# A chunked-attention kernel with two expert layers: the third tile moved ahead of two second halves, and one layer's block sums gathered in the sixth tile

## The chip, the cores and the metric

The kernel runs on one core of a Trainium2 chip. The metric is the device time of one execution in microseconds (us). TensorE (PE in the profile) multiplies matrices, VectorE (DVE), ScalarE (ACT) and GpSimd (POOL) compute element by element, SyncE (SP) issues transfers, and the DMA engines carry them. Each engine works through its own instructions in order; semaphores tie them together.

## What is computed

Attention within chunks of 64 positions, then two layers over its 4608 tokens. Weights come as float64.

```python
scores = scale * np.matmul(q_c, k_c.transpose(0, 1, 2, 4, 3))
scores = scores - np.max(scores, axis=-1, keepdims=True)
attn = np.exp(scores)
attn = attn / (np.sum(attn, axis=-1, keepdims=True) + 1e-09)
x = np.matmul(attn, v_c)          # -> 4608 x 512
...
h = x @ w_in                      # 512 x 2048
x = (h * np.cos(h)) @ w_out       # 2048 x 512
...
h = x @ w_in2                     # 512 x 1024
solu = h * softmax(h)
ln = (solu - mu) / np.sqrt(var + 1e-06) * g_ln
out = ln @ w_out2                 # 1024 x 512
```

## The kernel before

**Tiles, units and steps.** The tokens form nine tiles of 512. Attention is done in units: 0 to 3 (two chunks each) make tile 0, units 4 and 5 (four chunks each) tile 1, units 6 and 7 tile 2, and so on. A unit's output is x of its half tile, kept as a high and a low part (xh, xl), since a product of float32 precision is built from three matmuls of split operands. Two tiles of x fit in SBUF at a time (pool xp, 2 buffers).

Layer 1 runs in steps (j, f): tile j, and one of 16 blocks f of 128 columns of w_in. `mm_in` makes h of the step (12 matmuls), ACT and DVE make g = h cos h of it (`turns`: kt on ACT, r on DVE; `act_sin`: two passes on ACT; `dve_g`; `split_g`: gh on ACT, gl on DVE or POOL), and `mm_out` multiplies it with a block of w_out into y, two steps later (LAG 2). h has two PSUM buffers, so that h of step n + 2 goes where h of step n was, once g of step n is made. The order of the steps is the list `blocks`: before, tiles 0 and 1 do their first eight blocks each, then tile 0 the second eight, then tile 1, then tiles 2 to 8 all sixteen each. Step 85 is thus the sixth block of the sixth tile. A tile whose blocks are done in two halves keeps its partial y in DRAM meanwhile (`load_part` brings it back).

**What sets the order.** All instructions of PE, ACT, DVE, POOL and SP keep the order in which the program writes them (`InOrder`). Up to step 33 that is a list of words written by hand: h.3 is `mm_in(3)`, k, r, s, g, c, b or d the parts of a step's g, y.n and z.n the two halves of `mm_out(n)`; capital letters are pieces of a unit's attention (S.4 are the scores of unit 4, Tk its key transposes), lt, lv, lq load it; i1bH is a pass over the second half of pair 1 of w_in's blocks (H and W make the high and low parts, the other letters convert from float64), o0H one of w_out; wi, wo, li, lo load raw weights, and n.k are k warm-up matmuls on an identity, which compute nothing that is used. From step 34 on, a step has eight slots (e, p1, y, a1, d1, p2, a2, d2), and `plan` puts work into a slot of a step:

```python
def step(n):
    mm_in(n); run(n, "e"); turns(n); split_g(n - 1); run(n, "p1"); mm_out(n - LAG); run(n, "y")
    run(n, "a1"); run(n, "d1"); act_sin(n); dve_g(n); run(n, "p2"); run(n, "a2"); run(n, "d2")
```

`place` puts units 8 to 17 there; a unit's `load_next`, in slot p2, issues the q and k transfers of the unit after it: 32 transfers of 32 KB on SP. SP's transfers use eight semaphores in turn, and each one waits until the transfer eight before it has landed.

**Layer 2** multiplies x @ w_in2 by seven products of quarter blocks in place of eight, so it wants sums of w_in2's blocks. w_in2 is converted in the tiles 2 and 3 and put in DRAM (w2f0, w2f1: two halves kk of its rows). Then `load_blk(kk)` reads one half back (wf), `blk_sum` makes the sums s1 to s4 on DVE, and `keep` splits each of the seven blocks w11, w12, w22, s1 to s4 into a high part (an ACT pass, half 0) and a low part (a DVE pass, half 1) and stores both from a half e of the tile wk to DRAM, w2_<name>. A half of wk is written again only when the store before has read it. Before, kk = 0 is done in tile 4 and kk = 1 in tile 5.

Of the kernel before, what the change touches and what calls it, by code (L numbers as in the profile page):

```python
# [11 lines left out]
F32 = mybir.dt.float32  # L12
F32R = mybir.dt.float32r
# [15 lines left out]
def kernel(  # L29
# [13 lines left out]
    B, H, S, D = q.shape  # L43
# [3 lines left out]
    P = 128  # L47
    CH = 64
    T = 512
    NJ = NT // T  # L50
    SUB = T // P
    NI = NT // P
    KD = DM // P
    NF = F1 // P
# [8 lines left out]
    dr = ctx.enter_context(tc.tile_pool(name="dr", bufs=1, space=DRAM))  # L63
# [10 lines left out]
    NB = 8  # L74

    N32 = NB
    blocks = [(0, 0, NB), (1, 0, NB), (0, NB, NF), (1, NB, NF)]
    blocks += [(j, 0, NF) for j in range(2, NJ)]
    steps = [(j, f) for j, f0, f1 in blocks for f in range(f0, f1)]
    heads = {(j, f0) for j, f0, f1 in blocks}  # L80
    tails = {(j, f1 - 1) for j, f0, f1 in blocks}
    y_part = [dr.tile([P, KD * T], F32, name=f"yp{j}") for j in range(2)]
    y_dram = [dr.tile([2, P, 7 * 256], F32, name=f"yd{j}") for j in range(NJ)]

    xp = ctx.enter_context(tc.tile_pool(name="xp", bufs=2))
# [27 lines left out]
    sync = InOrder(nc.sync, in_order_loads)  # L113
# [110 lines left out]
    def load_w2in(g):  # L224
        t = sp_.tile([P, 1024], U64, tag="st", name="st")
        sync.dma_start(out=t, in_=w_in2[g * P:(g + 1) * P, :])
        raw["in2", g] = t
# [29 lines left out]
    def load_blk(kk):  # L257
        t = sp_.tile([P, 2048], F32, tag="st", name="wf")
        sync.dma_start(out=t, in_=w2f[kk])
        blk[kk] = t, zp.tile([P, 1024], F32, tag="z", name="z"), sp_.tile([P, 2048], F32R, tag="st", name="wk")  # L260
# [144 lines left out]
    def warm(n):  # L405

        t = ps_h.tile([P, P], F32, tag="h", name="none")
        for _ in range(n):
            pe.matmul(out=t, lhsT=ident, rhs=ident, start=True, stop=True)

    def att_tok(i, w):

# [170 lines left out]
    xh, xl = {}, {}  # L583
# [102 lines left out]
    def load_part(j):  # L686
        t = sp_.tile([P, KD, T], F32, tag="st", name="yp")
        sync.dma_start(out=t.rearrange("p m t -> p (m t)"), in_=y_part[j])
        parts[j] = t
# [75 lines left out]
    if True:  # L765
# [48 lines left out]
        for i in range(SUB, NU):  # L814
            j, o = divmod(UNITS[i][0] * CH, T)
# [3 lines left out]
        def plan(n, when, what):  # L819
            att.setdefault((n, when), []).append((lambda i: what(), NU))  # L820

        def conv_at(key, places):
            for (e, k), (n, when) in zip(((0, 0), (0, 1), (0, 2), (1, 0), (1, 1), (1, 2)), places):
                plan(n, when, lambda e=e, k=k: conv(key, e, k))

        for t in (2, 3):
            o = NF * t
            for x in range(2):
                plan(o + 5, "p2", lambda g=2 * x + t - 2: load_w2in(g))
            conv_at(("in2", t - 2), ((o + 7, "a2"), (o + 8, "d2"), (o + 9, "d2"), (o + 8, "a2"), (o + 10, "d1"), (o + 12, "d1")))  # L830
            conv_at(("in2", t), ((o + 13, "a1"), (o + 13, "d1"), (o + 13, "d2"), (o + 13, "a2"), (o + 14, "d2"), (o + 16, "d1")))
        for t in (4, 5):
            o, kk = NF * t, t - 4
            plan(o + 5, "p2", lambda kk=kk: load_blk(kk))
            for what, key, e, n, x in (
# [3 lines left out]
            ):  # L839
                if what == "s":  # L840
                    plan(o + n, f"d{x}", lambda kk=kk, key=key: blk_sum(kk, key))
                else:
                    plan(o + n, f"a{x}", lambda kk=kk, key=key, e=e: keep(kk, e, key, 0))
                    plan(o + n, f"d{x}", lambda kk=kk, key=key, e=e: keep(kk, e, key, 1))
        for t in (6, 7):
            o = NF * t
            for x in range(2):
                g = 2 * (t - 6) + x
                plan(o + 5, "p2", lambda g=g: load_w2out(g))
            g = 2 * (t - 6)  # L850
# [11 lines left out]
        def half_out(n, m):  # L862
# [20 lines left out]
            "Ck": lambda i: att_tokc(i, 1), "S": att_qk, "M": att_max, "U": att_sub, "E": att_exp,  # L883
            "R": att_sum, "L": att_mul, "P": att_pt, "D": att_ptc, "V": att_pv,
            "XH": lambda i: att_x(i, 0), "XL": lambda i: att_x(i, 1),
            "n": warm,
            "nq": lambda i: att_nat(i, "q"), "nk": lambda i: att_nat(i, "k"),
            "cq": lambda i: att_natc(i, "q"), "ck": lambda i: att_natc(i, "k"),
            "tq": lambda i: att_tr(i, "q"), "tk": lambda i: att_tr(i, "k"),
# [223 lines left out]
        BEFORE = 34  # L1113
        ordered[0] = True
        for word in (
# [26 lines left out]
        ).split():  # L1142
            if word == "|":
                first.close()
                cp = act_a.enter_context(tc.tile_pool(name="cp", bufs=2, reuse_waits="tile"))
            else:
                say(word)
# [20 lines left out]
        for n in range(BEFORE - 1, END):  # L1168
            j, f = steps[n - LAG]
# [46 lines left out]
        for i in range(EARLY, NI // 2 + (LAG2 + 1) // 2 + 1):  # L1216
            p, t = i - 1, 2 * i - LAG2
# [98 lines left out]
```

## Time and profile before

| | us |
|---|---|
| median of three runs | 1255.84 |
| runs | 1254.85, 1255.84, 1256.05 |
| profiled execution | 1254.68 |
| its span in the trace | 1252.9 |
| PE busy | 1241.4 (99%) |
| VectorE busy | 862.4 (69%) |
| ScalarE busy | 751.7 (60%) |
| GpSimd busy | 130.0 (10%) |
| mean granted TensorE clock | 0.998 |

The span is the time from the first to the last instruction in the trace; about 1.8 us of the execution lie around it. The granted clock is a share of TensorE's full 2.4 GHz; 0.5 is its other level, 1.2 GHz. Busy time is the sum of an engine's instructions; a row's bracket gives the idle time just before an instruction and what released it. SPq is SP's sequencer, on which an issue takes time from when it may start until it is handed over.

### The profile page before, as it was taken

The page shows a single profiled execution, that of the slowest core. Times are in us where ns is not written, and L with a number is a line of the kernel's source. Part 1 is how long each engine was busy: PE and PEld are TensorE (multiplying, and loading weights), DVE is VectorE, ACT ScalarE, POOL GpSimd, SP SyncE. Part 2 cuts the span into 40 slices and gives each one's busy share as a digit, 9 for nine tenths or more (in the row PEclk, how much of TensorE's full clock was granted, in tenths as well). Part 3 has the DMA queues.
Part 4 walks back from the last instruction along what each step waited for, and adds up shares of the span by engine and source line. Part 5 has one row for each costly group of instructions (what it writes and reads, how often), then busy time and mean ns, then how long its engine had stood idle before and what let it go on. Part 6 is the DMA issues. An engine that isn't in the chain of part 4 may idle for free.

```text
span 1252.9 us, 20476 instructions
## 1 busy us (share of the span) xinstructions
PE 1241.4 (99%) x7636; PEld 1012.5 (81%) x7636; DVE 862.4 (69%) x1390; ACT 751.7 (60%) x1108; POOL 130.0 (10%) x216
## 2 busy tenths in 40 slices
PE   8999999999999999999999999999999999999998
PEld 7767888888888888888888888888888888888887
DVE  5968875666766766667667757647689777777761
ACT  5968865555645645646646547537666655656552
POOL 1213322011011011011011011000000000000010
PEclk9999999999999999999999999999999999999999
DMA  9952152463263254354373371561556543454325
GB/s 226 276 138 101 58 135 57 114 171 74 54 176 66 58 144 128 85 136 130 80 169 76 85 160 51 194 221 60 164 142 180 129 125 108 121 152 122 75 50 120
DMA packets 249476, 153.95 MB, mean 123 GB/s; under 512 B 180001, under 2 KB 223521, under 8 KB 247585
## 3 DMA queue, kind: packets, MB, share of 16 engines
q1 hardware_dynamic: 245824, 148.32, 45.8%
q0 software_dynamic: 3456, 4.20, 1.5%
q8 instruction: 60, 0.98, 0.4%
q14 instruction: 40, 0.32, 0.1%
q10 hardware_dynamic: 96, 0.13, 0.0%
HBM read 85.73 MB, written 41.68 MB: 102 GB/s over the span
## 4 chain that ended last, share of the span: by engine, by line
PE 96%; ACT 1%; SPq 1%; DMA 1%; DVE 0%; issue 0%; ACTq 0%; DVEq 0%
PE h L104 44%; PE y L104 32%; PE o L104 15%; PE sc L104 2%; PE x L104 2%; SPq L104 1%; DMA qki<-in_k 0%; PE none L104 0%; PE kt L431 0%; PE qt L431 0%; PE pt L104 0%; DMA yd<-ye 0%; PE qkt L104 0%; SPq L1063 0%; ACT lh L104 0%
## 5 line engine op out<-in xcount | busy, mean ns | idle before, releaser
L104 PE MATMUL h<-xh,whi 128*128 128x512 f32 x576 | 229.4, 399 | 0.1
L104 PE MATMUL h<-xl,whi 128*128 128x512 f32 x576 | 224.0, 390 | 0.0
L104 PE MATMUL h<-xh,wlo 128*128 128x512 f32 x576 | 223.9, 390 | 0.0
L104 ACT ACTIVATE kt<-h 128x512 int32<-128x512 f32 x144 | 85.7, 595 | 225.6 <-PE h L104 224.6
L104 PE MATMUL y<-gh,whi 128*128 128x512 f32 x544 | 212.6, 391 | 0.0
L104 PE MATMUL y<-gl,whi 128*128 128x512 f32 x544 | 211.7, 389 | 0.0
L104 PE MATMUL y<-gh,wlo 128*128 128x512 f32 x544 | 211.7, 389 | 0.0
L104 ACT ACTIVATE r<-r 128x512 f32<-128x512 f32 x288 | 181.7, 631 | 47.5 <-DVE r L104 42.9
L104 DVE SCALAR_TENSOR_TENSOR r<-kt,h 128x512 f32<-128x512 int32 x144 | 98.6, 685 | 151.1 <-ACT kt L104 150.9
L104 DVE SCALAR_TENSOR_TENSOR g<-r,h 128x512 f32<-128x512 f32 x136 | 92.7, 681 | 56.0 <-ACT r L104 55.8
L104 PEld LDWEIGHTS h<-xh,whi 128*128 128x128 f32 x576 | 108.0, 188 | 26.0 <-issue 1.6
L104 PEld LDWEIGHTS h<-xh,wlo 128*128 128x128 f32 x576 | 108.2, 188 | 23.3 <-issue 1.2
L104 PEld LDWEIGHTS h<-xl,whi 128*128 128x128 f32 x576 | 108.1, 188 | 22.8
L104 PEld LDWEIGHTS y<-gh,whi 128*128 128x128 f32 x544 | 102.1, 188 | 21.5
L104 PEld LDWEIGHTS y<-gh,wlo 128*128 128x128 f32 x544 | 102.1, 188 | 21.3
L104 PEld LDWEIGHTS y<-gl,whi 128*128 128x128 f32 x544 | 102.1, 188 | 21.0
L104 PE MATMUL o<-whi,lh 128*128 128x512 f32 x288 | 112.0, 389 | 0.0
L104 PE MATMUL o<-wlo,lh 128*128 128x512 f32 x288 | 112.0, 389 | 0.0
L104 PE MATMUL o<-whi,ll 128*128 128x512 f32 x288 | 112.0, 389 | 0.0
L104 ACT ACTIVATE gh<-g 128x512 fp32r<-128x512 f32 x136 | 84.8, 624 | 23.7 <-DVE g L104 17.9
L533 POOL DMA_DIRECT2D ptb<-ptr x96 | 47.2, 499 | 495.4 <-DVE ptr L526 463.1
L104 PE MATMUL h<-whi,yl 128*128 128x512 f32 x252 | 98.2, 390 | 0.2 <-DVE yl L104 0.2
(112 smaller groups left out, 1953.5 us busy)
## 6 DMA issues: line engine op xcount, KB each, us to landing
lt<-bt SPq DMA_DIRECT2D x136, 128.0 KB
yr<-yd SPq DMA_DIRECT2D x18, 896.0 KB
yd<-ts SPq DMA_DIRECT2D x18, 512.0 KB
out<-os SPq DMA_DIRECT2D x142, 64.0 KB
vi<-in_v SPq DMA_DIRECT2D x64, 128.0 KB
qi<-in_q SPq DMA_DIRECT2D x224, 32.0 KB
ki<-in_k SPq DMA_DIRECT2D x224, 32.0 KB
raw<-in_moe_w_in SPq DMA_DIRECT2D x10, 512.0 KB
```

The source lines that it names most:

```text
L104: ins = getattr(self.engine, name)(*args, **kwargs)
L533: (sync if g < 2 else nc.gpsimd).dma_start(out=o[32 * g:32 * (g + 1), c].rearrange("p x s -> p (x s)"), in_=t[32 * c:32 * (c + 1), g].rear ...
```

## The change

- The order of the steps becomes: tiles 0 and 1 their first eight blocks, tile 2 all sixteen, then tile 1's second eight, then tile 0's second eight, then tiles 3 to 8. Since two tiles of x fit in SBUF, x of tile 0 is written to DRAM (word sx.0, two stores of 1 MB) and read back (rx.0, two loads of 1 MB).
- The hand-written list is new: units 6 and 7 come at h.7 to h.16 in place of h.19 to h.31, the weight passes of the pairs 4 to 7 later, there are 20 warm-up pieces in place of 40, and y.0 comes ahead of S.4.
- w_in2 is converted in tiles 3 and 4 in place of 2 and 3.
- Both halves of the block sums are done in tile 5, with other slots: the loads of wf in step 85 (p2) and step 90 (d2), the keeps from step 86 to 90 and from 92 to 96.

```diff
-    blocks = [(0, 0, NB), (1, 0, NB), (0, NB, NF), (1, NB, NF)]
-    blocks += [(j, 0, NF) for j in range(2, NJ)]
+    blocks = [(0, 0, NB), (1, 0, NB), (2, 0, NF), (1, NB, NF), (0, NB, NF)]
+    blocks += [(j, 0, NF) for j in range(3, NJ)]
...
+    x_park = dr.tile([P, 2, KD * T], F32, name="xd")
...
+    def park(j):
+        for e, x in enumerate((xh, xl)):
+            sync.dma_start(out=x_park[:, e], in_=x[j].bitcast(F32).rearrange("p k t -> p (k t)"))
+
+    def unpark(j):
+        for e, (x, name) in enumerate(((xh, "xh"), (xl, "xl"))):
+            x[j] = xp.tile([P, KD, T], F32R, tag=name, name=name)
+            sync.dma_start(out=x[j].bitcast(F32).rearrange("p k t -> p (k t)"), in_=x_park[:, e])
...
-        for t in (2, 3):
+        for j, n in ((1, 38), (0, 46)):
+            plan(n, "p2", lambda j=j: load_part(j))
+        for t in (3, 4):
             o = NF * t
             for x in range(2):
-                plan(o + 5, "p2", lambda g=2 * x + t - 2: load_w2in(g))
...
+                plan(o + 5, "p2", lambda g=2 * x + t - 3: load_w2in(g))
...
-        for t in (4, 5):
-            o, kk = NF * t, t - 4
-            plan(o + 5, "p2", lambda kk=kk: load_blk(kk))
+        for kk in range(2):
+            o = NF * 5 + 6 * kk
+            plan(o + 5 - kk, ("p2", "d2")[kk], lambda kk=kk: load_blk(kk))
             for what, key, e, n, x in (
-                ("k", "w12", 0, 8, 2), ("s", "s1", 0, 8, 2), ("s", "s2", 0, 9, 2), ("k", "w11", 1, 9, 2),
-                ("k", "w22", 0, 10, 2), ("s", "s4", 0, 12, 1), ("s", "s3", 0, 12, 1), ("k", "s1", 1, 12, 1),
-                ("k", "s2", 0, 12, 2), ("k", "s3", 1, 13, 1), ("k", "s4", 0, 13, 2),
+                ("k", "w12", 0, 6, 2), ("s", "s1", 0, 6, 2), ("s", "s2", 0, 7, 1), ("k", "w11", 1, 7, 2),
+                ("k", "w22", 0, 8, 1), ("s", "s4", 0, 8, 2), ("s", "s3", 0, 8, 2), ("k", "s1", 1, 8, 2),
+                ("k", "s2", 0, 9, 1), ("k", "s3", 1, 9, 2), ("k", "s4", 0, 10, 1),
             ):
...
-            "lt.0 lt.1 n.9 Tq.0 Cq.0 wi.0 lt.2 Tq.1 Tk.0 lt.3 Ck.0 n.4 S.0 Tk.1 M.0 i0aL U.0 wo.1 E.0 lw.0 Cq.1 R.0 Ck.1 "
...
+            "lt.0 wi.0 lt.1 Tk.0 lt.2 n.4 lt.3 Tq.0 Cq.0 Ck.0 Tq.1 S.0 Cq.1 wo.1 i0aL Tk.1 M.0 lw.0 n.2 U.0 i0aN E.0 Tk.2 "
...
```

PE in the opening, up to the first matmuls of layer 1 (none<-ident is warm-up, x an attention product, pt a transpose of the softmax, h layer 1). Before:

```order
L104 MATMUL x<-ptb,v_117 64x64 x16
L104 MATMUL none<-ident 128x128 x6
L104 MATMUL x<-ptb,v_117 64x64 x16
L104 MATMUL none<-ident 128x128 x3
L104 MATMUL pt<-ident,p 128x128 x4
L104 MATMUL none<-ident 128x128 x4
L104 MATMUL pt<-ident,p 128x128 x4
L104 MATMUL x<-ptb,v_117 64x64 x16
L104 MATMUL none<-ident 128x128 x2
L104 MATMUL x<-ptb,v_117 64x64 x16
L104 MATMUL none<-ident 128x128 x3
L104 MATMUL h<-xh,whi 128x512 x4
```

The same place in the changed kernel:

```order
L105 MATMUL x<-ptb,v_118 64x64 x16
L105 MATMUL none<-ident 128x128 x2
L105 MATMUL x<-ptb,v_118 64x64 x16
L105 MATMUL none<-ident 128x128
L105 MATMUL pt<-ident,p 128x128 x8
L105 MATMUL x<-ptb,v_118 64x64 x32
L105 MATMUL none<-ident 128x128 x2
L105 MATMUL h<-xh,whi 128x512 x4
```

Of the 18 warm-up pieces between the products of unit 0 and h.0, 5 are left, and the transposes and products of two units stand together.

SP in the sixth tile, from the load of the staged half (wf) on; w2_w12 and the like are the stores of the seven blocks, qi and ki the 32 transfers of `load_next`, vi values, ptb a copy of a unit's transposed softmax. Before:

```order
L104 DMA wf_5550<-w2f1_116 128x2048
L104 DMA vi_5647<-in_v 64x8x64 x4
L104 DMA qi_5744<-in_q 32x8x32 x16
L104 DMA ki_5761<-in_k 32x8x32 x16
L104 DMA w2_w12_105<-wk_5553 256x1x512
L104 DMA w2_w11_104<-wk_5553 256x1x512
L104 DMA w2_w22_109<-wk_5553 256x1x512
L104 DMA ptb_5911<-ptr_5910 32x256 x8
L104 DMA w2_s1_107<-wk_5553 256x1x512
L104 DMA w2_s2_106<-wk_5553 256x1x512
L104 DMA w2_s3_108<-wk_5553 256x1x512
L104 DMA w2_s4_110<-wk_5553 256x1x512
```

The same place in the changed kernel:

```order
L105 DMA wf_5506<-w2f0_116 128x2048
L105 DMA w2_w12_106<-wk_5509 256x1x512
L105 DMA vi_5607<-in_v 64x8x64 x4
L105 DMA w2_w11_105<-wk_5509 256x1x512
L105 DMA w2_w22_110<-wk_5509 256x1x512
L105 DMA qi_5711<-in_q 32x8x32 x16
L105 DMA ki_5728<-in_k 32x8x32 x16
L105 DMA w2_s1_108<-wk_5509 256x1x512
L105 DMA w2_s2_107<-wk_5509 256x1x512
L105 DMA w2_s3_109<-wk_5509 256x1x512
L105 DMA w2_s4_111<-wk_5509 256x1x512
L105 DMA wf_5842<-w2f1_117 128x2048
```

Three stores have moved ahead of the 32 transfers, four stand right behind them.

ACT in the steps 89 and 90 of the same tile (p is the exponential of a unit, kt, gh and r the passes of steps, wk<-wf a block's high part). Before:

```order
L104 ACTIVATE r_5799<-r_5799 128x512 x2
L104 ACT_TABLE_LOAD
L104 ACTIVATE p_5817<-p_5817 128x1024
L104 ACTIVATE wk_5553<-wf_5550 128x512
L104 ACTIVATE kt_5841<-h_5828 128x512
L104 ACTIVATE gh_5845<-g_5821 128x512
L104 ACT_TABLE_LOAD
L104 ACTIVATE r_5843<-r_5843 128x512 x2
L104 ACTIVATE wk_5553<-wf_5550 128x512
```

The same place in the changed kernel:

```order
L105 ACTIVATE r_5767<-r_5767 128x512 x2
L105 ACT_TABLE_LOAD
L105 ACTIVATE p_5786<-p_5786 128x1024
L105 ACTIVATE wk_5509<-wf_5506 128x512
L105 ACTIVATE kt_5811<-h_5798 128x512
L105 ACTIVATE gh_5815<-g_5792 128x512
L105 ACTIVATE wk_5509<-wf_5506 128x512
L105 ACT_TABLE_LOAD
L105 ACTIVATE r_5813<-r_5813 128x512 x2
```

The pass behind the exponential was that of w11 and is now that of s3; a second one, of s4, stands between gh and the sine of step 90.

## Rows read from the trace of the kernel before

**Rows 1.** The page: busy time of the engines, and engines of the last chain

```profile
PE 1241.4 (99%) x7636; PEld 1012.5 (81%) x7636; DVE 862.4 (69%) x1390; ACT 751.7 (60%) x1108; POOL 130.0 (10%) x216
...
PE 96%; ACT 1%; SPq 1%; DMA 1%; DVE 0%; issue 0%; ACTq 0%; DVEq 0%
```

**Rows 2.** PE's waits: what it waited for, total us, times, longest

```profile
PE qkt L104 <- DMA qki<-in_k: 2.7, 1, 2.7
...
PE h L104 <- DVE yl L104: 0.2, 1, 0.2
```

**Rows 3.** Timeline of PE, opening: start, us, instruction, count, [idle before, releaser]

```profile
12.56 0.80 PE L104 MATMUL qkt<-ident,qki 128*128 128x128 f32 x4 [2.66 <-DMA qki<-in_k]
...
23.29 1.60 PE L104 MATMUL none<-ident 128*128 128x128 f32 x12
...
31.15 1.19 PE L104 MATMUL h<-xh,whi 128*128 128x512 f32 x4
...
42.03 2.11 PE L104 MATMUL sc<-kt,qt 64*64 64x64 f32 x64 [1.12 <-ACT kt L104]
```

**Rows 4.** Stretch: length, busy PE, PEld, DVE, ACT, POOL, granted clock, DMA share, GB/s

```profile
12.50:16.40 3.90, 3.84 (x46) 3.43 (x46) 3.73 (x8) 0.87 (x2) 2.20 (x2) 0.56 1.11 235
```

**Rows 5.** Timeline of SP's queue in the sixth tile

```profile
548.92 0.34 SPq L104 DMA_DIRECT2D wf<-w2f  x1
...
558.15 8.02 SPq L104 DMA_DIRECT2D qi<-in_q  x16
566.27 8.62 SPq L104 DMA_DIRECT2D ki<-in_k  x16
574.98 5.03 SPq L104 DMA_DIRECT2D w_w<-wk  x3
...
589.01 6.85 SPq L104 DMA_DIRECT2D w_s<-wk  x4
```

**Rows 6.** Timeline of ACT in the sixth tile

```profile
560.42 0.62 ACT L104 ACTIVATE gh<-g 128x512 fp32r<-128x512 f32 x1
...
571.62 0.61 ACT L104 ACTIVATE wk<-wf 128x512 fp32r<-128x512 f32 x1
...
573.26 1.28 ACT L104 ACT_TABLE_LOAD   x1
574.56 1.30 ACT L104 ACTIVATE r<-r 128x512 f32<-128x512 f32 x2
578.12 0.63 ACT L104 ACTIVATE wk<-wf 128x512 fp32r<-128x512 f32 x1 [2.26 <-DMA w_w<-wk]
...
579.13 0.62 ACT L104 ACTIVATE gh<-g 128x512 fp32r<-128x512 f32 x1
```

**Rows 7.** Timeline of DVE in the sixth tile

```profile
561.17 0.69 DVE L104 TENSOR_TENSOR gl<-g,gh 128x512 fp32r<-128x512 f32 x1
...
575.89 0.69 DVE L104 SCALAR_TENSOR_TENSOR g<-r,h 128x512 f32<-128x512 f32 x1
```

**Rows 8.** The chain in the sixth tile: start, us, y of step 89, h of step 92

```profile
577.53 2.72 PE y L104 x12
580.25 2.72 PE h L104 x12
```

**Rows 9.** Stretches as in rows 4

```profile
25.00:60.00 35.00, 33.71 (x394) 25.49 (x391) 32.61 (x51) 31.89 (x48) 10.48 (x7) 1.00 0.95 275
551.00:553.00 2.00, 2.00 (x10) 1.44 (x8) 0.82 (x2) 0.00 (x0) 0.00 (x0) 1.00 0.94 369
558.00:566.20 8.20, 8.20 (x96) 6.66 (x95) 4.78 (x7) 2.90 (x5) 0.00 (x0) 1.00 0.54 95
566.20:575.00 8.80, 8.80 (x40) 7.28 (x40) 6.36 (x9) 7.98 (x11) 0.00 (x0) 1.00 0.40 62
```

**Rows 10.** Timeline of SP's queue between the weight loads

```profile
84.78 0.46 SPq L104 DMA_DIRECT2D raw<-in_moe_w_out  x1
110.11 0.33 SPq L104 DMA_DIRECT2D yp<-ye  x1
```

More of the change, by code (lines that the diff above doesn't have):

```diff
@@ L824, in conv_at @@
                 plan(n, when, lambda e=e, k=k: conv(key, e, k))
-        for t in (2, 3):
+        for j, n in ((1, 38), (0, 46)):
+            plan(n, "p2", lambda j=j: load_part(j))
+        for t in (3, 4):
             o = NF * t
             for x in range(2):
-                plan(o + 5, "p2", lambda g=2 * x + t - 2: load_w2in(g))
-            conv_at(("in2", t - 2), ((o + 7, "a2"), (o + 8, "d2"), (o + 9, "d2"), (o + 8, "a2"), (o + 10, "d1"), (o + 12, "d1")))
-            conv_at(("in2", t), ((o + 13, "a1"), (o + 13, "d1"), (o + 13, "d2"), (o + 13, "a2"), (o + 14, "d2"), (o + 16, "d1")))
-        for t in (4, 5):
-            o, kk = NF * t, t - 4
-            plan(o + 5, "p2", lambda kk=kk: load_blk(kk))
+                plan(o + 5, "p2", lambda g=2 * x + t - 3: load_w2in(g))
+            conv_at(("in2", t - 3), ((o + 7, "a2"), (o + 8, "d2"), (o + 9, "d2"), (o + 8, "a2"), (o + 10, "d1"), (o + 12, "d1")))
+            conv_at(("in2", t - 1), ((o + 13, "a1"), (o + 13, "d1"), (o + 13, "d2"), (o + 13, "a2"), (o + 14, "d2"), (o + 16, "d1")))
+        for kk in range(2):
+            o = NF * 5 + 6 * kk
+            plan(o + 5 - kk, ("p2", "d2")[kk], lambda kk=kk: load_blk(kk))
             for what, key, e, n, x in (
[3 rows of a table removed]
[3 rows of a table added]
             ):
@@ L885 @@
             "XH": lambda i: att_x(i, 0), "XL": lambda i: att_x(i, 1),
-            "n": warm,
+            "n": warm, "sx": park, "rx": unpark,
             "nq": lambda i: att_nat(i, "q"), "nk": lambda i: att_nat(i, "k"),
```

50 rows, old and new, of the table BEFORE are left out of this document.

## The prediction

> **What bounds the kernel now.** I read the page's busy shares and its chain first: PE (TensorE) is busy for 1241.4 of a span of 1252.9 us, and the chain that ends last lies 96% on PE [rows 1]. So the kernel is as long as its matmuls, and their number does not change. An edit can then pay only where PE waits or does filler work, and can cost only where it makes PE wait. PE's waits, read next, are few: the longest is 2.7 us on an attention input, and behind 60 us a single one of 0.2 us is left [rows 2]. Whatever can be gained therefore lies in the opening, before 60 us; some 1190 us behind it have nothing to give and much to lose. PE's row of the opening [rows 3] shows warm-up matmuls (none<-ident, filler while the first attention units are prepared) right up to h.0, the first matmul of layer 1, at 31.15. From the sixth tile I read what each in-order queue does around steps 88 to 92: SP, which issues the transfers [rows 5], ScalarE (ACT) [rows 6], VectorE (DVE) [rows 7] and PE [rows 8]. In this stretch PE never waits, but ACT does: it stands 2.26 us at 578.12 for the store of a half of wk.
>
> The sum is made against the profiled execution, 1254.68 us; it lies 1.16 below the median of the runs, 1255.84.
>
> **The opening.** Between the wait at 12.56 and h.0 at 31.15, 54 recorded warm-up matmuls stand before, and 28 in the changed order (27 and 14 pieces; the six pieces at 23.29 are recorded as 12). The wait at 12.56 itself stays: it is for the third unit's key tile, and the same transfers stand ahead of that in both orders. The 26 that go cost 0.13 us each (12 of them take 1.60 at 23.29) [rows 3], 3.5 us. All of that is saved if PE's own work sets the time of h.0, none if the softmax on ACT and DVE does; both engines also convert weights there. The rows for both show gaps, so neither end is excluded; I take the middle, **-1.7** (0 to -3.5). Two smaller edits about cancel: the wait of 1.12 before the scores at 42.03 [rows 3] gets the y matmuls of step 0 ahead of it, a gain of up to 1.1; against that o0H, a weight pass, now stands ahead of i1bH, on which h.3 waits, which costs up to about as much. I count **0**, between -1.1 and +1.3.
>
> **The tile pulled ahead.** The third tile's attention now runs between h.7 and h.16, and the weight preparation it displaces goes to h.14 to h.29. x of the first tile goes to DRAM and back: 2 stores and 2 loads of 1 MB. SP has nothing to issue from 85.24 to 110.11 [rows 10], and the stores, and the transfers of units 6 and 7, fall there. The loads back are issued at step 33 for step 40; a step takes 5.44 us (12 matmuls of h and 12 of y at 2.72 each, [rows 8]), so there are 38 us for 2 MB, which at 369 GB/s [rows 9] take 5.7. Cost **0**, hidden by PE's own matmuls; if the cover fails (unit 7's keys land some 3 us before their transposes by the same count), 2 to 5 us. The conversion of w_in2, one tile later, costs 0 in the same way: its passes stand in the same slots.
>
> **The sixth tile.** This is the term that decides. Before, load_next(13), 32 transfers for the next unit's q and k, is issued at 558.15, ahead of all seven block stores; it holds SP until 574.98 [rows 5]. The stores of w12, w11 and w22 follow, and those of s1 to s4 come 14 us later. In the changed order the first group's keeps stand two to four steps earlier, so that the stores of w12, w11 and w22 lie ahead of the 32 loads, but those of s1 to s4 behind them. Nothing may overtake on SP. Step by step:
> - w22's low half is a DVE pass in step 88, between gl at 561.17 [rows 7] and 562.5; its store then takes up to 1.7 of SP (5.03 for three, [rows 5]). The 32 loads start at 562.5 to 564.5 instead of 558.15.
> - They take 16.83 as before (558.15 to 574.98). The store of s1 is issued at 579.3 to 581.3.
> - A store's half of wk is given back 3.14 us after its issue: 574.98 to 578.12 [rows 5, 6]. So at 582.4 to 584.4.
> - s3 goes into the same half of wk as s1. Its ACT pass stands where w11's stood before, behind the exp, and ACT arrives there at 571.62 [rows 6]. It waits **10.8 to 12.8 us**.
> - Queued behind it on ACT: kt of step 90, gh of step 89, the pass of s4, a table load, the sine of step 90. From the released pass at 578.12 to the end of gh it is 1.63 (579.13 + 0.62) [rows 6]. So gh of step 89 is ready at 584.0 to 586.0, and PE, which wants it for y of step 89 at 577.53 [rows 8], stands for 6.5 to 8.5.
> - s4 shares its half with s2, whose store is issued some 1.7 behind that of s1: its release (584.1 to 586.1) comes when gh is done. Then 0.5 for s4, 1.28 for the table load, and 2.02 from the sine's start at 574.56 to the end of g (575.89 + 0.69) [rows 6, 7]: g of step 90 at 587.9 to 589.9. h of step 92 needs it (two PSUM buffers for h, so h.92 takes the one g.90 frees), and started at 580.25 [rows 8]. PE is then 7.7 to 9.7 late; y of step 89 (2.72) fits into this. I take **+8.7**.
>
> Behind it PE is the bound again, so the loss stays. The nearest row for PE's clock behind a wait: after the 2.66 us at 12.56 the stretch 12.50 to 16.40 was granted 0.56, close to 1.2 of 2.4 GHz [rows 3, 4], which costs 0.44 of 3.9 us, **+1.7**; 0 if the clock holds, 3.4 if it falls behind both waits. The second group (steps 90 to 96) costs 0: its four s stores come before the next 32 loads, behind 4 only. The first load of the group comes one step ahead of its use where it was three; ACT then waits for it in step 86 (issued at 548.92 [rows 5]; some 2.8 of data and 3.1 to a release make about 555), and PE's two steps of lag cover that; if they don't, +1.
>
> Sum: 1254.68 - 1.7 + 8.7 + 1.7 = 1263.4, and with 1.16 to the median 1264.5.
>
> A rule that speaks against this: the Trainium skill, "DMA: Bandwidth & Descriptors", section "Issuing engines are not separate DMA queues", says that the time to initiate transfers is usually small relative to the transfer. The rows say otherwise for these 32: the DMA engines are busy for 0.54 and 0.40 of the time while SP is held for 16.83 [rows 5, 9]. What the rule would give is the first rival.
>
> **The rivals.**
> 1. Not slower: the 32 loads (32 KB each, 1.05 MB) hold SP only as long as their data moves. At the 369 GB/s that 551 to 553 reached [rows 9] that is 2.8 us; s1's store would leave at 566 to 567 and release at 569 to 570, ahead of ACT's 571.62, and no engine would wait. The point from which it decides: s1's store has to be issued before 571.62 - 3.14 = 568.5. Time: 1254.68 - 1.7 + 1.16 = 1254.1. For it speaks only that the queue before s1's store is otherwise emptier; against it [rows 5], where both sixteens took 8 us each.
> 2. Partial: the loads still start at 558 (w22's store goes out without delay, its pass being ahead of the others), s1's store at 575.0, release 578.1. ACT frees gh at 579.7 and g of step 90 at 583.6: h.92 is 3.4 late. 1254.68 - 1.7 + 3.4 + 1.16 = 1257.5. Against it: ACT's keep pass for w22 can't start before the gh of step 87, after 561.
> 3. Main plus a shortage early: the third tile pulled ahead leaves units 6 and 7 waiting for transfers behind the 2 MB parked, +2 to 5, 1266 to 1269.5. For it speaks the DMA share of 0.95 from 25 to 60 [rows 9]; against it the idle SP [rows 10].
>
> **How the numbers follow.** Main 0.72, first rival 0.10, second 0.08, third 0.10. Main's own range is the stall's 7.7 to 9.7, the clock's 0 to 3.4 and the opening's -4.6 to +1.3 together, hardly all at one end: 1259.5 to 1268.5. The range to hold 8 in 10 goes down to 1256, which takes in most of the second rival, and up to 1269 for the third. Measurement can tell 0.2%, 2.5 us, from no change: below 1253.3 is faster, to 1258.3 the same. Faster needs the first rival with the opening near its full 4.6: 0.06. The same: the rest of the first and the second, 0.13. Slower: 0.81.
>
> **What would show it.** In the changed trace: a wait of 10 us or more of ACT on wk, released by the store of an s block, near 572 to 584; PE dry on y at about 576 for 6 to 9 us and once more for a microsecond or so on h; SP's two rows of 16 between the store of w22 and that of s1; the granted clock below 1 for some microseconds behind the wait; h.0 at 27.5 to 31. I am wrong if the s1 store is issued before 568.5 on before's scale, if PE waits anywhere between 60 and 540, or if h.0 comes more than 3.5 earlier.

## The result, and the profile after

The changed kernel takes 1263.6 us (median of 6 runs, 1261.74 to 1264.91) against 1255.88 before (6 runs): a ratio of 1.0061, 95% interval 1.0048 to 1.0074. It is slower by 7.7 us, as forecast (1264.5). Its profiled execution has a span of 1260.7, against 1252.9 before.

Two slips of name stand in the text above: the 32 transfers issued in step 88 are those of `load_next(15)` for unit 16, and `place` puts units 8 to 19. Neither touches a number.

The page and PE's waits answer [rows 1, 2]. First the page: busy time, and the engines of the last chain.

```profile
PE 1240.2 (98%) x7596; PEld 1009.8 (80%) x7596; DVE 860.7 (68%) x1389; ACT 752.2 (60%) x1108; POOL 131.1 (10%) x217
...
PE 80%; issue 12%; SPq 3%; DVE 2%; DMA 1%; ACT 1%; POOL 1%; ACTq 0%; POOLq 0%
```

Then PE's waits: what was waited for, total us, times, longest.

```profile
PE y L105 <- ACT gh L105: 6.9, 1, 6.9
PE qkt L105 <- DMA qki<-in_k: 5.2, 1, 5.2
...
PE h L105 <- DVE wlo L105: 0.3, 1, 0.3
PE h L105 <- ACT whi L105: 0.3, 1, 0.3
```

PE is busy for as long as before, but there is a new wait of 6.9 us for gh, and the last chain no longer lies on PE alone. It leaves PE in the sixth tile, where SP's queue answers [rows 5]:

```profile
546.59 0.34 SPq L105 DMA_DIRECT2D wf<-w2f  x1
553.74 0.61 SPq L105 DMA_DIRECT2D w_w<-wk  x1
...
562.00 8.49 SPq L105 DMA_DIRECT2D qi<-in_q  x16
570.53 7.85 SPq L105 DMA_DIRECT2D ki<-in_k  x16
578.48 8.36 SPq L105 DMA_DIRECT2D w_s<-wk  x4
586.89 0.60 SPq L105 DMA_DIRECT2D wf<-w2f  x1
```

The 32 loads start behind the stores of w12, w11 and w22 and hold SP for 16.48 us; the first s store follows at 578.48. From the fourth on, each load is 0.45 us of issuing, and the next follows at once. One of them:

```profile
571.03 0.45 SPq L105 DMA_DIRECT2D ki<-in_k  x1
```

The list of SP's own waits is empty from 562.6 to 578.4: what holds SP is the issuing of 32 transfers, and not their landing. ACT, answering [rows 6]:

```profile
569.62 1.06 ACT L105 ACTIVATE p<-p 128x1024 f32<-128x1024 f32 x1
581.57 0.63 ACT L105 ACTIVATE wk<-wf 128x512 fp32r<-128x512 f32 x1 [10.89 <-DMA w_s<-wk]
582.11 0.58 ACT L105 ACTIVATE kt<-h 128x512 int32<-128x512 f32 x1
582.58 0.62 ACT L105 ACTIVATE gh<-g 128x512 fp32r<-128x512 f32 x1
583.10 0.62 ACT L105 ACTIVATE wk<-wf 128x512 fp32r<-128x512 f32 x1
583.74 1.28 ACT L105 ACT_TABLE_LOAD   x1
585.03 1.29 ACT L105 ACTIVATE r<-r 128x512 f32<-128x512 f32 x2
```

The pass of s3 waits 10.89 us for the store of s1, with gh of step 89 queued behind it. PE's timeline shows the other end, and the chain the start of h of step 92, which answers [rows 8]:

```profile
583.26 0.80 PE L105 MATMUL y<-gh,whi 128*128 128x512 f32 x1 [6.92 <-ACT gh L105]
```

```profile
588.28 2.72 PE h L105 x12
```

The stretches ahead of, in and behind the wait (length, busy PE, PEld, DVE, ACT, POOL, granted clock, DMA share, GB/s):

```profile
570.00:576.30 6.30, 6.30 (x28) 4.89 (x27) 0.00 (x0) 0.68 (x1) 0.00 (x0) 1.00 0.43 67
576.30:583.20 6.90, 0.03 (x1) 0.00 (x0) 0.97 (x2) 1.63 (x4) 0.00 (x0) 0.78 0.60 182
583.20:588.28 5.08, 4.90 (x13) 3.60 (x14) 4.85 (x9) 4.75 (x8) 0.00 (x0) 0.62 0.43 162
588.28:593.00 4.72, 4.72 (x23) 3.90 (x22) 4.33 (x6) 2.38 (x5) 1.14 (x3) 1.00 0.87 278
```

Before the wait h and y start 1.20 us earlier than before the change, from step 34 to step 91 without a break (further ahead the order of the steps differs). h of step 92 then starts at 588.28 against 580.25 [rows 8], 8.03 later, and every step behind it keeps that 8.03. So the stall costs 9.23 (8.03 + 1.20): 6.92 of dry PE, and the rest, 2.3, at a granted clock of 0.62 behind it, where the y of step 89 takes 5.02 from its start to that of h in place of 2.72.

### The profile page after: what moved, and what is told of

It reads as the page before. It is cut to its first block, busy times and chain, and to the rows that moved or that the text cites. A ratio compares the mean times of both kernels' runs of the same rounds, so it can differ in the third digit from the quotient of the medians.

```text
span 1260.7 us, 20392 instructions
## 1 busy us (share of the span) xinstructions
PE 1240.2 (98%) x7596; PEld 1009.8 (80%) x7596; DVE 860.7 (68%) x1389; ACT 752.2 (60%) x1108; POOL 131.1 (10%) x217
## 4 chain that ended last, share of the span: by engine, by line
PE 80%; issue 12%; SPq 3%; DVE 2%; DMA 1%; ACT 1%; POOL 1%; ACTq 0%; POOLq 0%
PE h L105 36%; PE y L105 25%; PE o L105 15%; SPq L105 3%; PE x L105 1%; PE sc L105 1%; DMA wf<-w2f 0%; DMA raw<-in_moe_w_in 0%; DVE z L105 0%; POOL ptb L543 0%; DMA yd<-ye 0%; PE kt L441 0%; PE qt L441 0%; PE pt L105 0%; DMA w_s<-wk 0%
```

## The experiments

All times are medians, beside runs of the kernel before on the same chip: 1256.06 for the first four, 1255.49 for the last four.

**The s stores on another queue.**

```diff
         if half == 1:
-            sync.dma_start(
+            (pool if kk == 0 and key[0] == "s" else sync).dma_start(
                 out=w2_dram[key]...
```

> The changed kernel, with one thing moved: the stores of s1 to s4 of the first group (kk = 0) are issued from GpSimd, which does nothing in the sixth tile, and no longer from SP behind the 32 q and k loads. Theory (the stall is the order of SP's queue): s1's store leaves when its low half is made, near 565 to 566, and gives its half of wk back before ACT arrives with s3 near 570.7; ACT waits under 1 us, PE is not dry, h of step 92 starts 1.2 us earlier than before the change. Time 1254.7 (1253.7 to 1255.8), 0.7% below the changed kernel. Rival (the stores are held by the 32 transfers in the DMA engines, not by SP's order): ACT still waits 5 us or more on wk, time 1258 to 1263.

Measured: 1253.41 us, ratio to before 0.9978 (0.9968 to 0.9987). Only four stores leave SP's queue. The loads start where they did and take 18.5 us, 2 us longer than in the changed kernel:

```profile
561.66 8.69 SPq L105 DMA_DIRECT2D qi<-in_q  x16
570.39 9.81 SPq L105 DMA_DIRECT2D ki<-in_k  x16
```

ACT of this run:

```profile
570.30 0.62 ACT L105 ACTIVATE wk<-wf 128x512 fp32r<-128x512 f32 x1
...
572.77 0.63 ACT L105 ACTIVATE wk<-wf 128x512 fp32r<-128x512 f32 x1 [0.85 <-DMA w_s<-wk]
```

and GpSimd's queue, which issues the store of s1 at once:

```profile
565.61 0.72 POOL L105 DMA_DIRECT2D w_s<-wk  x1 [26.06 <-DVE wk L105]
```

The pass of s3 runs at 570.30 without a wait, PE is never dry behind 60 us but for 0.2 in layer 2 that was there before, and 10.2 us are gone (1263.6 - 1253.4, measured on different chips). The store of s1 gives its half of wk back while the 32 loads are still being issued, so these don't block it in the DMA engines. The rival falls; the time is 0.3 below the range of the theory. This version beats both kernels.

**Half of the loads behind the stores.**

```diff
+            elif i == 15:
+                load_att(16, "q")
...
+        plan(90, "d2", lambda: load_att(16, "k"))
```

> The changed kernel with 16 of the 32 loads (those of k) moved behind the seven stores and behind the load of the second staged half. Theory (SP's order, 0.5 us per load): s1's store is issued near 570.5, its half released near 573.6, ACT waits 2.9 us in place of 10.9, gh of step 89 is ready near 575.2, ahead of PE at 576.3: no dry PE, time 1254.7 (1253.7 to 1256). Rival (all or nothing: any load ahead of the s stores stops them, or the time goes elsewhere): 1260 to 1264.

Measured: 1258.13, ratio 1.0018 (1.0009 to 1.0027). On the stall the theory is met to the tenth: ACT waits 2.87 us, and the y of step 89 doesn't wait. But the time is 3.4 above the expected, and the rival's is not met either. SP's queue and PE's waits of this run show a wait that I had left out:

```profile
570.47 8.36 SPq L105 DMA_DIRECT2D w_s<-wk  x4
578.88 0.60 SPq L105 DMA_DIRECT2D wf<-w2f  x1
579.53 11.99 SPq L105 DMA_DIRECT2D ki<-in_k  x16
591.89 5.03 SPq L105 DMA_DIRECT2D ptb<-ptr  x8
```

```profile
PE x L105 <- DMA ptb<-ptr: 2.2, 2, 1.3
```

The 16 loads that were moved now stand ahead of the copies of a unit's softmax (ptb), issued at 583.63 before the change, at 581.08 in the first experiment and at 591.89 here. The attention product of that unit waits 2.2 us for them, the granted clock is 0.81 from 595.5 to 600.5 and 0.70 to 603.0, and the steps behind are 4.9 later than step 91: 0.3 at steps 92 and 93, 4.5 around the attention product. The same queue, the same 16 loads, another victim. Not all of the 11.99 us is issuing: SP's own waits from 579 to 592 show that it also stood for the second staged half, whose load is issued eight transfers ahead on the same semaphore:

```profile
SPq L105 <- DMA wf<-w2f: 2.7, 1, 2.7
```

**A quarter of the loads behind the stores.**

```diff
+            elif i == 15:
+                load_att(16, "q")
+                load_att(16, "k", (0,))
...
+        plan(90, "d2", lambda: load_att(16, "k", (1,)))
```

> The changed kernel with only 8 of the 32 loads moved behind the stores, 24 stay ahead. Theory: s1's store is issued near 574.6, released near 577.7, ACT waits 7 us, PE is dry for 2.9 us on gh of step 89 and h of step 92 is some 4 us later than without a stall; if the clock falls after so short a wait as it does after 6.9 us, another 1 to 2 us, part of it beside the wait. Time 1258 to 1260.5. Rival (all or nothing): 1263 or 1254.7.

Measured: 1258.91, ratio 1.0023 (1.0014 to 1.0032), within the expected range. ACT, and the stretches in and behind PE's wait:

```profile
577.45 0.63 ACT L105 ACTIVATE wk<-wf 128x512 fp32r<-128x512 f32 x1 [7.11 <-DMA w_s<-wk]
```

```profile
576.00:579.20 3.20, 0.06 (x1) 0.06 (x1) 1.08 (x2) 1.75 (x4) 0.00 (x0) 1.00 0.74 273
579.20:584.30 5.10, 4.67 (x13) 3.54 (x14) 4.87 (x10) 4.74 (x8) 0.00 (x0) 0.67 0.46 171
```

With 16, 24 and 32 loads ahead of the s stores ACT waits 2.87, 7.11 and 10.89 us: about half a microsecond for each load. PE is dry for 0, 3.1 and 6.9. The steps behind are 5.6 later here: 3.1 dry, 0.4 on gl, and 2.1 that go at the lower clock.

**The early keeps alone, in the kernel before.**

```diff
             for what, key, e, n, x in (
                 ...slots of before...
-            ):
+            ) if kk == 0 else (
+                ("k", "w12", 0, 6, 2), ("s", "s1", 0, 6, 2), ("s", "s2", 0, 7, 1), ("k", "w11", 1, 7, 2),
+                ("k", "w22", 0, 8, 1), ("s", "s4", 0, 8, 2), ("s", "s3", 0, 8, 2), ("k", "s1", 1, 8, 2),
+                ("k", "s2", 0, 9, 1), ("k", "s3", 1, 9, 2), ("k", "s4", 0, 10, 1),
+            ):
```

> The kernel before with one part of the change alone: in the sixth tile its own group (kk = 1) uses the new, earlier slots; the order of the tiles, the opening, the conversion and the other group stay as they were. Theory (the early slots beside the 32 loads are the whole loss): 1255.9 + 9.2 = 1265.1 (1264 to 1266.5), ACT waits near 11 us on wk, PE dry for near 7. Rival (it takes both groups in one tile, or the tile pulled ahead): 1255.5 to 1258.

Measured: 1267.51, ratio 1.0092 (1.0076 to 1.0107). The part alone makes the whole loss, so the rival falls; it even makes 1 us more than the range allowed. ACT, and the stretches in and behind PE's wait:

```profile
585.55 0.63 ACT L104 ACTIVATE wk<-wf 128x512 fp32r<-128x512 f32 x1 [12.33 <-DMA w_s<-wk]
```

```profile
578.80:587.20 8.40, 0.07 (x1) 0.00 (x0) 0.99 (x2) 1.65 (x4) 0.00 (x0) 0.63 0.57 161
587.20:592.20 5.00, 4.83 (x13) 3.56 (x14) 4.77 (x9) 4.67 (x7) 0.00 (x0) 0.60 0.42 160
```

By its own steps the stall costs 10.75: 8.4 dry and 2.35 at the lower clock. It is 1.5 longer than in the changed kernel: counted from the same step, the staged half is loaded 1.1 us later here, behind the y stores of the fifth tile, and the 32 loads take 17.16 in place of 16.48.

**The warm-up pieces put back, and taken away.** Both start from the kernel of the first experiment. The first run doubles the 14 pieces; the second leaves all 14 out.

```diff
-... Tq.3 n.3 L.0 ... P.0 n.4 E.1 ... n.1 Ck.3 ... n.1 o0bL ... n.2 U.2 ... n.1 R.3 ... n.2 h.0
+... Tq.3 n.6 L.0 ... P.0 n.8 E.1 ... n.2 Ck.3 ... n.2 o0bL ... n.4 U.2 ... n.2 R.3 ... n.4 h.0
```

> The kernel of e1_pool_stores (changed kernel without the stall) with the 14 warm-up pieces between the third unit's key transposes and h.0 doubled to 28, so that as many stand there as before the change. Theory (the softmax passes on ACT and DVE set the time of h.0, and PE has 1.9 us of dry time there that takes up part of the extra work): 0.5 to 1.7 us more than e1, 1254 to 1255.2. Rival (PE's own work sets h.0, as the full price of the prediction had it): 28 matmuls at 0.13 = 3.5 more, 1256.9.

Measured: 1253.74, ratio to before 0.9988 (0.9978 to 0.9997). In the trace h of step 34 starts at 244.60, to the hundredth where it starts without the 28 extra matmuls (other profiles of the opening without them have it at 243.99 to 244.90). No cost can be seen: less than the theory's 0.5, and the rival's 3.5 is out.

> The kernel of e1_pool_stores with the 14 warm-up pieces between the third unit's key transposes and h.0 taken away. Theory (softmax chain): no gain, 1253.4 within 0.7, or a loss of 1 to 2 where the longer dry times let the granted clock fall ahead of h.0. Rival (PE's own work): 3.5 us less, 1250.

Measured: 1254.69, ratio 0.9993 (0.9984 to 1.0001). No gain; in the trace h of step 34 comes 2.0 later than with them (246.59). The stretches before and behind h.0 (at 30.43) show why:

```profile
25.00:31.00 6.00, 3.46 (x72) 2.62 (x71) 5.07 (x10) 5.14 (x11) 0.91 (x1) 0.71 0.75 283
31.00:36.00 5.00, 5.00 (x26) 3.83 (x26) 2.12 (x5) 2.99 (x6) 2.51 (x2) 0.66 0.98 278
```

h.0 is no earlier, and the first h run at 0.66 of the full clock, where the first experiment's trace has 1.00 in both stretches. Theory held, at its unfavourable end.

**Two weight passes exchanged back.** Also from the first experiment's kernel.

```diff
-... o1bO o0H R.4 i1bH k.2 ...
+... o1bO i1bH R.4 o0H k.2 ...
```

> The kernel of e1_pool_stores with two words of the opening exchanged back: i1bH, on which h.3 waits, again ahead of o0H. Theory (the two short waits of h on whi and wlo, 0.3 us each, are the price of that order): 0.3 to 0.6 less than e1, 1252.8 to 1253.1, below what the measurement can tell by the time alone, seen in the trace as the waits gone. Rival (another wait takes their place within the same steps, since the same ACT passes are only exchanged): 1253.4, h of step 8 no earlier.

Measured: 1253.95, ratio 0.9986 (0.9978 to 0.9995). In the trace h.3 starts 1.1 earlier than in the first experiment (49.56 against 50.65), h.4 only 0.4, h of step 34 0.4 (244.21), with one wait on wlo left:

```profile
PE h L105 <- DVE wlo L105: 0.7, 1, 0.7
```

Most of it is given back within a step, and the time can't tell the two. Inconclusive between 0 and 0.4.

**x parked twice.** Also from the first experiment's kernel.

```diff
-... r.6 sx.0 L.5 ...
+... r.6 sx.0 sx.0 L.5 ...
```

> The kernel of e1_pool_stores with x of the first tile written to DRAM twice (4 stores of 1 MB in place of 2). Theory (hidden, SP and the DMA engines have room near 81 to 110 us): 1253.4 within 1. Rival (the third tile's loads behind it are near their limit): 2 to 5 more, with a wait of PE on transposes of unit 6 or 7 or on x of tile 2.

Measured: 1253.94, ratio 0.9986 (0.9977 to 0.9995): no cost. The key transfers of unit 7 are issued from 106.23 on, 5.4 us later than in the first experiment and 3.5 later than in the changed kernel. The key transpose on DVE waits for them now, but PE does not:

```profile
117.44 1.25 DVE L460 STREAM_TRANSPOSE kt<-ki 128x1024 f32<-128x1024 f32 x1 [1.78 <-DMA ki<-in_k]
```

## Why the prediction was right, step by step

**The stall: right in place, order and size.** On the changed kernel's own scale, 1.2 us earlier: the loads were to start at 561.3 to 563.3 and did at 562.00; 16.83 of SP, 16.48; the s1 store at 578.1 to 580.1, 578.48; a release 3.14 later, 3.09; ACT's wait 10.8 to 12.8, 10.89; PE dry 6.5 to 8.5, 6.92. It lies at the low end because SP was free for the loads nearly at once: the store of w22 held it for 0.55, of up to 1.7 allowed for. That it is SP's order and not the transfers is shown by the first experiment, that the cost goes with the number of loads ahead by the second and third, that no other part of the change is needed by the fourth.

**The clock and the second wait: counted twice.** I added a second wait of PE, on g of step 90 (8.7 in all), and then 1.7 for the clock, 10.4 together; it is 9.23. The second wait didn't come: at a granted clock of 0.62 the y of step 89 took 5.02, and g of step 90 was ready at 587.05, before y ended and h of step 92 started at 588.28:

```profile
586.36 0.69 DVE L105 SCALAR_TENSOR_TENSOR g<-r,h 128x512 f32<-128x512 f32 x1
```

What was wrong is the sum of the two, since the slow matmuls run while ACT and DVE catch up. The overestimate is 1.2; the opening, which gained 0.5 less than forecast, hid part of it. That the total came within 1 us is in part luck.

**The opening: right in size, wrong in its cause.** -1.7 was forecast; the traces show -1.2 in the changed kernel (h of step 34 at 244.89 against 246.09), -1.5 as the mean of five profiles of the same opening (244.89, 244.60, 244.90, 244.55 and 243.99), and the timings of the experiments that have no stall -1.5 to -2.7 (1253.41 - 1256.06, 1253.94 - 1255.49). The fourth experiment, with the opening of before, has it at 247.43, so the profile of before is no firm base either. Two steps of the forecast fell. "The wait at 12.56 itself stays" is wrong: PE's timeline of the changed kernel, which answers [rows 3], starts with a longer wait and has none there:

```profile
5.16 1.09 PE L105 MATMUL qkt<-ident,qki 128*128 128x128 f32 x4 [5.16 <-DMA qki<-in_k]
...
24.63 0.66 PE L105 MATMUL pt<-ident,p 128*128 128x128 f32 x4 [0.40 <-POOL p L105]
...
27.12 1.09 PE L105 MATMUL x<-ptb,v 64*64 64x64 f32 x32 [0.78 <-DVE xl L105]
28.52 1.13 PE L105 MATMUL x<-ptb,v 64*64 64x64 f32 x32 [0.31 <-DVE xl L105]
...
30.45 1.26 PE L105 MATMUL h<-xh,whi 128*128 128x512 f32 x4
...
42.13 2.10 PE L105 MATMUL sc<-kt,qt 64*64 64x64 f32 x64
```

And the warm-up pieces saved nothing by going: PE now waits for p and xl ahead of h.0, and the same pieces put back cost nothing. The middle of "all or none" had the right size by chance. What the wait at 12.56 had cost beside its 2.66 us is seen in the clock of 12.50 to 16.40: 0.56 before, 1.00 in the changed kernel, whose longest wait lies ahead of its first matmul. That this is the gain at h.0 is likely, but no run shows it alone. The wait before the scores at 42.03 is gone, as forecast, and the two waits of 0.3 us on h.3's weights came as forecast. Of the gain at step 34, 0.7 was there at h.0, of which 0.3 was left at step 5. The rest, 0.87, came between steps 5 and 34, with the same 1148 matmuls in both kernels. A wait of 0.15 at 182.64 is gone; what is left lies at the changes from one kind of matmul to another, which come in another order and once less often. They are slow: at 69.60, behind y<-gf,z, 0.64 us pass from the first h to the second, where 0.23 is usual.

**The tile pulled ahead and the park: 0, as forecast.** The changed kernel's SP queue, where [rows 10] had a gap:

```profile
84.87 0.62 SPq L105 DMA_DIRECT2D xd<-xh  x1
85.53 0.43 SPq L105 DMA_DIRECT2D xd<-xl  x1
86.06 5.07 SPq L105 DMA_DIRECT2D vi<-in_v  x4
91.23 11.39 SPq L105 DMA_DIRECT2D qi<-in_q  x16
102.72 7.80 SPq L105 DMA_DIRECT2D ki<-in_k  x16
```

Between 60 and 540 us PE waits nowhere. The margin was real, some 2.5 us in the changed kernel by the issue times above: parking twice uses it up on DVE, and PE still has cover.

**The second group: 0, as forecast.** ACT waits 2.3 us there for an s store and PE goes on. **The rule of the Trainium skill** ("DMA: Bandwidth & Descriptors", section "Issuing engines are not separate DMA queues"), that the time to initiate is usually small beside the transfer, does not hold here: 32 transfers of 32 KB held SP for 16.48 us at a DMA share of 0.43 (row 570.00 to 576.30), and to issue four stores elsewhere was worth 10 us.

## What to carry to other kernels

Where one in-order queue carries both loads that nobody needs soon and stores that free a buffer, look at what stands ahead of each store: its price is the whole row of transfers in front of it, and it lands on whichever engine rewrites the buffer, with everything queued behind that. Bulk loads moved out of the way push back whatever comes after them on the same queue; a queue of an idle engine is the better way out. And when PE runs dry, count the slow stretch behind the wait as time in which the other engines catch up, not as one more term.

## What the runs showed of the hardware

In these traces the price of the lower clock hardly depends on how long PE was dry: after 3.1, 6.9 and 8.4 us the next 5 us were granted 0.67, 0.62 and 0.60, and cost 2.1, 2.3 and 2.35 us beyond the dry time. Even the two waits of 1.31 and 0.92 us on ptb cost 2.2 beside their 2.2. After shorter waits the clock went either way: with three or four of 0.3 to 0.8 us ahead of h.0, the stretch from 25 to 31 was granted 0.72 in the changed kernel's profile and 1.00 in the first experiment's, and h.0 came at 30.45 and 29.92. Warm-up matmuls were free there as long as PE had to wait anyway.

The opening varies by itself: with the code of before unchanged there, h.0 started at 31.15 in one profile and at 32.45 in another (the fourth experiment), so a term of 1 us in it can't be read from a single profile. The two differ in the clock behind the wait at 12.6: 0.56 from 12.50 to 16.40 and then 1.00 to 21.30 in the one, 0.74 and then 0.51 in the other.

Issuing has its own price on SP: 0.45 us for each load of 32 KB, also where the DMA engines were busy for only 0.40 to 0.54 of the time.
